# A second buffer for the turned block of an attention read, paid for with a buffer of the block it is made from

## The chip, the cores and the metric

The kernel runs on one core of one Trainium2 chip. The metric is the device time of one execution in microseconds (us). Before the change it is 499.29 us, the median of three runs (498.58 to 499.64). The engines are named as in the profile: PE is TensorE's matmul, PEld its weight load, DVE is VectorE, ACT is ScalarE, SP is SyncE, which here only issues transfers (SPq is its queue).

## What is computed

There are 8 batches with 8 heads, 512 tokens of 64 elements per head, and a state of 32 rows per head. Tokens read the state and the state reads the tokens, both by softmax attention; the 544 rows of each batch, with 512 columns, then go through a bilinear pair of weights and two more.

```python
scores = scale * np.matmul(x, state.transpose(0, 1, 3, 2))
a = np.exp(scores - scores.max(-1, keepdims=True)); a /= a.sum(-1, keepdims=True) + 1e-09
xread = np.matmul(a, state)
scores2 = scale * np.matmul(state, x.transpose(0, 1, 3, 2))
a2 = np.exp(scores2 - scores2.max(-1, keepdims=True)); a2 /= a2.sum(-1, keepdims=True) + 1e-09
sread = np.matmul(a2, x)
...
a = x @ w1
b = x @ w2
h = a * b @ w3
return (h @ w_out).astype(np.float32)
```

In the last four lines `x` is the concatenation of `xread` and `sread`, 8 x 544 rows of 512. Everything is float32.

## The kernel before

Each float32 operand of the large products is split in two parts that the matmul takes (`split`, lines 94 to 99: ACT writes the high part, DVE the low part), and a product is three matmuls, low by high, high by high, high by low.

**Prologue** (lines 510 to 617): the weights are loaded and converted, `w3` and `w_out` are multiplied into one matrix `wo`, and batch 0 is computed as the weights arrive. Batch 0's second stage runs at lines 622 to 630, with steps of batch 1's attention put between its pieces, among them the read of batch 0 (`reads[0]`). In the same stretch `combine_weights` (lines 362 to 373) is called four times, the last time at line 501 inside batch 1. It makes `t_hi` and `t_lo`, sums and differences of quarters of `wo`: two additions (L366), four subtractions (L372), then a split.

**Batches 1 to 7** (`quarter_batch`, lines 479 to 502): the first stage has eight groups, ft 0 to 7. Each is 12 matmuls of 128x512 (L311, in `stage1_sums`) into a pair of PSUM banks from the pool `ps_2`, which has three such pairs. ACT copies one half of the pair to SBUF (L487) and DVE multiplies the copy by the other half (L394). That multiplication is the last reader of the pair, so a later group can only start when it is done. Then the second stage (`stage2_quarters`, lines 427 to 477) makes seven products (L421) of the quarters, with the next batch's `sw` tiles (L147 and a split) between them.

**The attention of the next batch** runs inside a batch. After group ft = 1 (line 489) come, in this order: the read of the state for this batch (`read_state`, lines 234 to 257), the scores of the next batch (L147 into a `ps_2` pair that is held until its maximum, L190, its transposition, L187, and its exponentials, L197, are done), and the loads of the tokens of the next batch and of the x of the one after it (L159, L153, L155). The softmax's later steps are L204 to L228.

**The read of the state**, which the change touches: 64 small matmuls (L243) give a block of 128x128; DVE divides it by the softmax sum into the tile `scaled` (L248), transposes its 32x32 squares into the tile `turned` (L252), and 16 transfers of 4 KB on SP's queue (L171, `move_blocks`) carry `turned` into `sread`, 32 rows at a time. `sread` is used only at the end, in `state_rows`. The tiles come from the pool `att`, which has two buffers for each name unless `bufs=1` is given. So `scaled` had two buffers in turn and `turned` had one: a batch's transposition could write `turned` only after the 16 transfers of the batch before had read it.

**What sets the order.** PE's and SP's instructions run in the order in which they are written. From batch 0 on DVE and ACT are put in order when the kernel is built, by a scheduler that places instructions by its own estimate of when they can start. On the chip each engine's instructions start in the order that was built. On SP's queue the 16 transfers of batch 0's `turned` stand behind the 16 that move the softmax of batch 1 (`e<-work`, L171), although `turned` is written before; right behind them stand the 16 of batch 1's `turned`, and behind those the three loads.

Of the kernel before, what the change touches and what calls it, by code (L numbers as in the profile page):

```python
# [22 lines left out]
F32 = mybir.dt.float32  # L23
# [6 lines left out]
P = 128  # L30
# [9 lines left out]
def attn_bilinear_kernel(  # L40
# [11 lines left out]
    B, _, NT, H, D = x_s.shape  # L52
# [3 lines left out]
    KT = H * NS // P  # L56
# [10 lines left out]
    att = ctx.enter_context(tc.tile_pool(name="att", bufs=2))  # L67
# [20 lines left out]
    def bank():  # L88
        return ps_o.tile([P, NF], F32, name="ps_o")

    def two_banks():
        return ps_2.tile([P, 2, NF], F32, name="ps_2")

    def split(hi, lo, src):

        return (
            nc.scalar.copy(out=hi, in_=src),  # L97
            nc.vector.tensor_tensor(out=lo, in0=src, in1=hi.bitcast(F32), op=ALU.subtract),  # L98
        )
# [41 lines left out]
    def per_head(ps, b, moving):  # L141


        for j in range(NP):
            for q in range(KT):
                rows = slice(q * D, (q + 1) * D)
                nc.tensor.matmul(  # L147
                    ps[j * NS:(j + 1) * NS, q], sts[b][rows, j], moving(rows, j), start=True, stop=True
                )
# [14 lines left out]
    def work_tile():  # L164
        return att.tile([P, KT, S], F32, name="work")

    def move_blocks(dest, src):

        for j in range(NP):
            for c in range(P // NS):  # L170
                nc.sync.dma_start(  # L171
                    out=dest(slice(c * NS, (c + 1) * NS), j), in_=src(slice(j * NS, (j + 1) * NS), c)
                )

    def attention_steps(b):
        xd = x_tiles[b]
        a2 = {}

        def scores():

            ps = two_banks()
            per_head(ps, b, lambda rows, j: xd[rows, j])
            yield
            flat = lambda t: t.rearrange("p k s -> p (k s)")

            s1 = work_tile()
            nc.vector.transpose(out=flat(s1), in_=flat(ps))  # L187

            m2 = att.tile([P, KT], F32, name="m2")
            nc.vector.tensor_reduce(out=m2, in_=ps, axis=AX.X, op=ALU.max)  # L190
            nc.vector.tensor_scalar_mul(m2, m2, -SCALE)
            e2 = att.tile([P, KT, S], F32, name="e2", bufs=1)
            sum2 = att.tile([P, KT], F32, name="sum2")
            a2["e"], a2["sum"] = e2, sum2
            for kt in range(KT):
                one = slice(kt, kt + 1)
                nc.scalar.activation(  # L197
                    out=e2[:, kt], in_=ps[:, kt], func=AF.Exp, bias=m2[:, one], scale=SCALE, accum_out=sum2[:, one]
                )

            J = KT * S // NS
            s1v = flat(s1).rearrange("p (j n) -> p j n", n=NS)
            m1 = att.tile([P, J], F32, name="m1")
            nc.vector.tensor_reduce(out=m1, in_=s1v, axis=AX.X, op=ALU.max)  # L204
            nc.vector.tensor_tensor(
                out=s1v, in0=s1v, in1=m1.unsqueeze(2).broadcast_to([P, J, NS]), op=ALU.subtract
            )
            nc.scalar.activation(out=s1, in_=s1, func=AF.Exp, scale=SCALE)
            yield
            nc.vector.tensor_scalar_add(sum2, sum2, 1e-9)  # L210
            nc.vector.reciprocal(out=sum2, in_=sum2)
            sum1 = att.tile([P, J], F32, name="sum1")
            nc.vector.tensor_reduce(out=sum1, in_=s1v, axis=AX.X, op=ALU.add)
            nc.vector.tensor_scalar_add(sum1, sum1, 1e-9)
            nc.vector.reciprocal(out=sum1, in_=sum1)
            nc.vector.tensor_tensor(
                out=s1v, in0=s1v, in1=sum1.unsqueeze(2).broadcast_to([P, J, NS]), op=ALU.mult
            )
            yield
            at = work_tile()  # L220
            nc.vector.transpose(out=flat(at), in_=flat(s1))
            at_tiles[b] = [att.tile([P, KT, S], F32R, name=f"at_{part}", bufs=1) for part in ("hi", "lo")]
            last = split(*at_tiles[b], at)
            yield

            blocks = work_tile()
            with tc.issue_after(last[1].ins):
                nc.vector.transpose(out=flat(blocks), in_=flat(e2))  # L228
            a2["t"] = work_tile() if b < PLAIN else att.tile([P, KT, S], F32, name="e2", bufs=1)
            tiles = lambda t: t.rearrange("p k (t m) -> p (k t) m", m=P)  # L230
            move_blocks(lambda its, j: tiles(a2["t"])[its, :, j * NS:(j + 1) * NS],
                        lambda mine, c: tiles(blocks)[mine, :, c * NS:(c + 1) * NS])

        def read_state():

            xs = token_tiles[b]

            ps = (bank() if b else two_banks()[:, 0])[:, :KT * D].rearrange("p (k d) -> p k d", k=KT)
            for kt in range(KT):
                for t in range(NT):  # L240
                    for j in range(NP):
                        mine = slice(j * NS, (j + 1) * NS)
                        nc.tensor.matmul(  # L243
                            ps[mine, kt], a2["t"][:, kt, t * P + j * NS:t * P + (j + 1) * NS],
                            xs[:, t, 2 * j + kt], start=(t == 0), stop=(t == NT - 1),
                        )
            scaled = att.tile([P, KT, D], F32, name="scaled")
            a2["read"] = nc.vector.tensor_tensor(  # L248
                out=scaled, in0=ps, in1=a2["sum"].unsqueeze(2).broadcast_to([P, KT, D]), op=ALU.mult
            )  # L250
            turned = att.tile([P, KT, D], F32, name="turned", bufs=1)
            nc.vector.transpose(  # L252
                out=turned.rearrange("p k d -> p (k d)"), in_=scaled.rearrange("p k d -> p (k d)")
            )
            yield
            move_blocks(lambda its, j: sread[its, j, b * NS:(b + 1) * NS],
                        lambda mine, c: turned.rearrange("p k (c n) -> p (k c) n", n=NS)[mine, c])

        return scores, read_state, a2


# [446 lines left out]
```

## Time and profile before

| what | us |
|---|---|
| median of three runs (range) | 499.29 (498.58 to 499.64) |
| the profiled execution, its own time | 499.09 |
| its span in the trace | 497.3 |
| PE busy | 488.3 |
| DVE busy | 376.2 |
| ACT busy | 238.6 |

The span is the time from the first to the last instruction in the trace; 1.79 us of the profiled execution lie around it. All times within a trace count from the start of the span. A row of a timeline gives start, duration, engine, line, operation and tiles; a bracket at its end gives the idle time of the engine just before it and what ended that. In a row of waits stand who waited, for whom, the total, the number of times and the longest. Matmuls are pipelined: a 128x512 one is drawn 0.39 us long, and the next starts about 0.23 us after it.

### The profile page before, as it was taken

How to read it: one execution, taken by the hardware profiler on the slowest of the kernel's cores; microseconds unless marked ns; L12 is line 12 of the kernel's file. 1: busy time of each engine (PE TensorE's matmuls, PEld its weight loads, DVE VectorE, ACT ScalarE, POOL GpSimd, SP SyncE). 2: the span in 40 equal slices, each digit the busy share in tenths (PEclk: the TensorE clock that was granted, in tenths of full speed). 3: DMA queues.
4: the chain of work that ended last, by engine and by line, in shares of the span. 5: the costliest groups of instructions: out<-in, count | busy, mean ns of one | idle time of the engine just before them, and what ended most of it. 6: DMA issues, size and time to landing. Idle time of an engine off the chain costs nothing.

```text
span 497.3 us, 8933 instructions
## 1 busy us (share of the span) xinstructions
PE 488.3 (98%) x3558; PEld 379.4 (76%) x3558; DVE 376.2 (76%) x555; ACT 238.6 (48%) x364; POOL 0.2 (0%) x4
## 2 busy tenths in 40 slices
PE   8999999999989999999999999999999999999996
PEld 6444467777667978797879787978897789899885
DVE  5669896798689769956994799479938983577770
ACT  4777884454256225813570357045605550454650
POOL 0000000000000000000000000000000000000000
PEclk9999999999989999999999999999999999999999
DMA  8995971063013314140404041304130213001101
GB/s 341 366 415 198 368 267 30 13 217 73 21 48 133 81 51 144 44 99 25 176 12 119 5 178 33 97 4 176 44 86 5 88 44 84 6 3 47 39 2 42
DMA packets 56362, 52.50 MB, mean 106 GB/s; under 512 B 42752, under 2 KB 50944, under 8 KB 51712
## 3 DMA queue, kind: packets, MB, share of 16 engines
q1 hardware_dynamic: 47488, 43.27, 26.3%
q10 hardware_dynamic: 8832, 8.65, 5.1%
q8 instruction: 28, 0.46, 0.4%
q14 instruction: 14, 0.11, 0.1%
HBM read 38.27 MB, written 8.91 MB: 95 GB/s over the span
## 4 chain that ended last, share of the span: by engine, by line
PE 78%; DVE 10%; SPq 6%; ACT 3%; DMA 2%; issue 1%; DVEq 0%; ACTq 0%
PE ps L311 29%; PE ps_o L421 25%; SPq L171 6%; PE ps L147 6%; PE ps L421 4%; PE ps L647 3%; PE ps_o L528 3%; PE ps L528 3%; PE ps_o L325 3%; PE ps L648 2%; DVE w_sb L134 1%; PE ps_o L243 1%; DMA raw<-in_w_k_dram 1%; DVE sw_lo L98 1%; DVE w_sb L130 1%
## 5 line engine op out<-in xcount | busy, mean ns | idle before, releaser
L311 PE MATMUL ps<-at_lo,sw_hi 128*128 128x512 f32 x256 | 102.5, 401 | 3.4 <-DVE g_x L394 3.4
L311 PE MATMUL ps<-at_hi,sw_hi 128*128 128x512 f32 x256 | 100.4, 392 | 0.0
L311 PE MATMUL ps<-at_hi,sw_lo 128*128 128x512 f32 x256 | 100.3, 392 | 0.0
L487 ACT COPY tmp<-ps 128x512 f32<-128x512 f32 x56 | 32.8, 586 | 126.0 <-PE ps L311 71.8
L311 PEld LDWEIGHTS ps<-at_lo,sw_hi 128*128 128x128 f32 x256 | 48.4, 189 | 21.7 <-DVE g_x L394 11.0
L311 PEld LDWEIGHTS ps<-at_hi,sw_lo 128*128 128x128 f32 x256 | 48.4, 189 | 10.4
L311 PEld LDWEIGHTS ps<-at_hi,sw_hi 128*128 128x128 f32 x256 | 48.5, 190 | 9.7 <-issue 0.2
L394 DVE TENSOR_TENSOR g_x<-tmp,ps 128x512 f32<-128x512 f32 x28 | 19.1, 684 | 33.3 <-ACT tmp L487 32.8
L98 DVE TENSOR_TENSOR sw_lo<-ps,sw_hi 128x1024 fp32r<-128x1024 f32 (+1 forms) x34 | 38.0, 1151 | 0.2 <-ACT sw_hi L97 0.2
L97 ACT CAST g_hi<-g_x 128x512 fp32r<-128x512 f32 x42 | 26.0, 621 | 21.2 <-PE ps_o L421 13.1
L421 PE MATMUL ps_o<-t_lo,g_hi 128*128 128x256 f32 x168 | 34.5, 287 | 0.0
L421 PE MATMUL ps_o<-wo_lo,g_hi 128*128 128x256 f32 x168 | 34.4, 286 | 0.0
L421 PE MATMUL ps_o<-wo_hi,g_hi 128*128 128x256 f32 x168 | 33.8, 283 | 0.0
L421 PE MATMUL ps_o<-t_hi,g_hi 128*128 128x256 f32 x168 | 33.8, 283 | 0.0
L421 PE MATMUL ps_o<-wo_hi,g_lo 128*128 128x256 f32 x168 | 33.8, 283 | 0.0
L421 PE MATMUL ps_o<-t_hi,g_lo 128*128 128x256 f32 x168 | 33.8, 283 | 0.0
L97 ACT CAST g_hi<-raw 128x512 fp32r<-128x512 f32 x42 | 25.1, 619 | 16.8 <-DVE raw L394 7.7
L98 DVE TENSOR_TENSOR g_lo<-raw,g_hi 128x512 fp32r<-128x512 f32 x42 | 28.6, 687 | 5.1 <-ACT g_hi L97 4.8
L97 ACT CAST sw_hi<-ps 128x1024 fp32r<-128x1024 f32 (+1 forms) x34 | 31.1, 966 | 1.7 <-PE ps L147 1.6
L147 PE MATMUL ps<-w_sb,st 64*32 64x512 f32 (+1 forms) x544 | 31.4, 570 | 0.0
L421 PEld LDWEIGHTS ps_o<-wo_lo,g_hi 128*128 128x128 f32 x168 | 26.6, 191 | 5.6 <-ACT tmp L446 5.0
L421 PEld LDWEIGHTS ps_o<-t_lo,g_hi 128*128 128x128 f32 x168 | 26.1, 192 | 5.0 <-issue 5.0
(109 smaller groups left out, 895.3 us busy)
## 6 DMA issues: line engine op xcount, KB each, us to landing
raw<-in_w_k_dram SPq DMA_DIRECT2D x8, 1024.0 KB, 6.9
x_d<-in_x_d_dram SPq DMA_DIRECT2D x8, 1024.0 KB, 7.5
raw<-in_w_dram SPq DMA_DIRECT2D x8, 1024.0 KB, 6.3
x_s<-in_x_s_dram SPq DMA_DIRECT2D x8, 1024.0 KB, 5.1
out_dram<-tmp ACTq DMA_DIRECT2D x56, 128.0 KB, 1.8
raw<-in_w3t_dram SPq DMA_DIRECT2D x4, 1024.0 KB, 6.6
e<-work SPq DMA_DIRECT2D x112, 32.0 KB, 2.0
sread<-turned SPq DMA_DIRECT2D x128, 4.0 KB, 1.7
```

The costliest lines, as they stand in the source:

```text
L97: nc.scalar.copy(out=hi, in_=src),
L98: nc.vector.tensor_tensor(out=lo, in0=src, in1=hi.bitcast(F32), op=ALU.subtract),
L147: nc.tensor.matmul(ps[j * NS:(j + 1) * NS, q], sts[b][rows, j], moving(rows, j), start=True, stop=True)
L171: nc.sync.dma_start(out=dest(slice(c * NS, (c + 1) * NS), j), in_=src(slice(j * NS, (j + 1) * NS), c))
L311: nc.tensor.matmul(ps[:, i], w[:, kt, c:c + P], a[:, kt], start=(k == 0), stop=(k == 3 * KT - 1))
L325: nc.tensor.matmul(ps[:, :DO], g, wo[w][:, ft, :], start=(ft == 0 and k == 0), stop=(ft == FT - 1 and k == 2))
L394: nc.vector.tensor_tensor(out=whole, in0=a, in1=b, op=ALU.mult)
L421: nc.tensor.matmul(ps[:, tt * HO:(tt + 1) * HO], g[:, tt * P:(tt + 1) * P], w(part, k), start=(fresh and k == 0 and n == 0 and tt == 0), s ...
L487: nc.scalar.copy(out=a_sb, in_=ps[:, 0])
L528: nc.tensor.matmul(w34_ps[i][:, :DO], chunks[k][:, DO + i * P:DO + (i + 1) * P], w_out[k], start=(k == 0), stop=(k == FT - 1),)
L647: nc.tensor.matmul(ps[:, i], wh[:, ks], sr[:, kt], start=(kt == 0), stop=False)
L648: nc.tensor.matmul(ps[:, i, :n], wl[:, ks], sr[:, kt, 1], start=False, stop=(kt == NP - 1))
```

## The change

`scaled` gets one buffer instead of two and `turned` two instead of one. Both are blocks of 128x128 float32, so the pool takes as much room as before.

```diff
@@ read_state @@
-            scaled = att.tile([P, KT, D], F32, name="scaled")
+            scaled = att.tile([P, KT, D], F32, name="scaled", bufs=1)
             a2["read"] = nc.vector.tensor_tensor(
                 out=scaled, in0=ps, in1=a2["sum"].unsqueeze(2).broadcast_to([P, KT, D]), op=ALU.mult
             )
-            turned = att.tile([P, KT, D], F32, name="turned", bufs=1)
+            turned = att.tile([P, KT, D], F32, name="turned")
             nc.vector.transpose(
```

No instruction is added or taken away. On PE, ACT and SP the built order is the same as before, with the same waits. On DVE one instruction moves and the waits on transfers change.

The first place is on DVE in batch 1, from the last split before the read to the product of group ft = 3. `ps_1058` is the scores of batch 2, `ps_1084` and `ps_1114` are the banks of ft = 2 and ft = 3, and `[waits ...]` names the semaphores that an instruction waits for (DMAHW0 to DMAHW7 count transfers). Before:

```order
L98 TENSOR_TENSOR g_lo<-tmp,g_hi 128x512 [waits Activation_49]
L366 TENSOR_TENSOR tmp<-wo_hi,wo_lo 128x512 [waits DMAHW6_49]
L366 TENSOR_TENSOR tmp<-wo_hi,wo_lo 128x512 [waits DMAHW1_49]
L372 TENSOR_TENSOR raw<-tmp 128x256 [waits DVE_49] x2
L372 TENSOR_TENSOR raw<-tmp,raw 128x256 [waits DVE_49]
L187 STREAM_TRANSPOSE work<-ps_1058 128x1024 [waits PE_49]
L394 TENSOR_TENSOR g_x<-tmp,ps_1084 128x512 [waits Activation_49]
L252 STREAM_TRANSPOSE turned<-scaled 128x128 [waits DMAHW4_49,DMAHW5_49,DMAHW3_49,DMAHW6_49,DMAHW2_49,DMAHW7_49,DMAHW1_49,DMAHW0_49]
L372 TENSOR_TENSOR raw<-tmp,raw 128x256 [waits DVE_49]
L190 TENSOR_REDUCE m_1103<-ps_1058 128x2
L98 TENSOR_TENSOR t_lo<-raw,t_hi 128x4x256 [waits Activation_49]
L394 TENSOR_TENSOR g_x<-tmp,ps_1114 128x512 [waits Activation_49]
```

And after:

```order
L98 TENSOR_TENSOR g_lo<-tmp,g_hi 128x512 [waits Activation_49]
L252 STREAM_TRANSPOSE turned<-scaled 128x128 [waits DVE_49]
L366 TENSOR_TENSOR tmp<-wo_hi,wo_lo 128x512 [waits DMAHW6_49]
L366 TENSOR_TENSOR tmp<-wo_hi,wo_lo 128x512 [waits DMAHW1_49]
L372 TENSOR_TENSOR raw<-tmp 128x256 [waits DVE_49] x2
L372 TENSOR_TENSOR raw<-tmp,raw 128x256 [waits DVE_49]
L187 STREAM_TRANSPOSE work<-ps_1058 128x1024 [waits PE_49]
L394 TENSOR_TENSOR g_x<-tmp,ps_1084 128x512 [waits Activation_49]
L372 TENSOR_TENSOR raw<-tmp,raw 128x256 [waits DVE_49]
L190 TENSOR_REDUCE m_1103<-ps_1058 128x2
L98 TENSOR_TENSOR t_lo<-raw,t_hi 128x4x256 [waits Activation_49]
L394 TENSOR_TENSOR g_x<-tmp,ps_1114 128x512 [waits Activation_49]
```

The transposition L252 has moved seven instructions up, ahead of the last `combine_weights` and of the product of ft = 2, and waits for DVE's own `scaled` alone; the wait on all eight counts of transfers in front of L372 is gone.

The second place is on DVE later in batch 1, where the softmax of batch 2 is transposed back (L221). The piece of the difference:

```order
 L98 TENSOR_TENSOR g_lo_1307<-raw_1151,g_hi_1306 128x512
 L98 TENSOR_TENSOR sw_lo_1275<-ps_2_1265,sw_hi_1274 128x1024 [waits Activation_49]
-L221 STREAM_TRANSPOSE work_1338<-work_1101 128x1024
+L221 STREAM_TRANSPOSE work_1338<-work_1101 128x1024 [waits DMAHW4_49,DMAHW3_49,DMAHW5_49,DMAHW2_49,DMAHW7_49,DMAHW1_49,DMAHW0_49]
 L98 TENSOR_TENSOR g_lo_1391<-g_x_973,g_hi_1390 128x512 [waits PE_49,Activation_49]
 L98 TENSOR_TENSOR g_lo_1393<-g_x_1099,g_hi_1392 128x512 [waits PE_49,Activation_49]
```

Nothing moves here, but L221 now names seven counts of transfers itself, which the wait at L252 had covered for it before. In batches 2 to 7 L252 stands where it stood, without its waits on transfers.

## Prediction, on record before the run

> **What bounds the kernel now.** I read the page first, then the busy time by batch, then the waits, and last the timelines round the one wait that the change can touch.
>
> ```profile
> PE 488.3 (98%) x3558; PEld 379.4 (76%) x3558; DVE 376.2 (76%) x555; ACT 238.6 (48%) x364; POOL 0.2 (0%) x4
> ```
>
> PE is busy for 98% of the span, so time can be won only where PE idles or runs slowly. The busy time of each engine from one batch's read of the state (L243) to the next shows where that is; the columns after the stretch are its length, then busy us and instructions of PE, PEld, DVE, ACT and POOL, and PE's granted clock.
>
> ```profile
> 125.27:179.01 53.74, 50.39 (x413) 41.34 (x416) 41.46 (x62) 21.97 (x36) 0.00 (x0) 0.97 0.25 73
> 179.01:227.67 48.66, 48.66 (x413) 40.24 (x416) 38.01 (x55) 21.54 (x35) 0.00 (x0) 1.00 0.26 79
> 227.67:276.34 48.67, 48.67 (x412) 40.23 (x416) 37.92 (x55) 21.44 (x35) 0.00 (x0) 1.00 0.26 80
> ```
>
> Batch 1, the first row, issues the same matmuls as batch 2 and takes 53.74 us for 48.66, or 5.08 us more, with a clock below 1. That is a ceiling: nothing that mends batch 1 alone gains more. The list of waits says what ended its idle time.
>
> ```profile
> DVE turned L252 <- DMA sread<-turned: 2.8, 1, 2.8
> PE ps L311 <- DVE g_x L394: 3.4, 1, 3.4
> ```
>
> Only one of the eight transpositions into `turned` waited for the transfers of the batch before, for 2.8 us; and PE waited once for a product L394, for 3.4 us. The chain of waits joins the two.
>
> ```profile
> 133.75 1.72 DMA sread<-turned
> ...
> 135.59 0.31 DVE turned L252
> 135.90 0.31 DVE raw L372
> 136.21 1.14 DVE m L190
> 137.34 1.20 DVE t_lo L98
> 138.54 0.61 DVE g_x L394
> ...
> 139.20 10.06 PE ps L311 x36
> ```
>
> The last of batch 0's 16 small transfers lands, L252 runs, and four more DVE instructions stand between it and the product of group ft = 3 (L394), which frees the PSUM pair for group ft = 5. PE, at 139.20, starts that group.
>
> **The change part by part: the wait.** Here is DVE's timeline at that place.
>
> ```profile
> 132.11 0.65 DVE L394 TENSOR_TENSOR g_x<-tmp,ps 128x512 f32<-128x512 f32 x1
> 135.59 0.31 DVE L252 STREAM_TRANSPOSE turned<-scaled 128x128 f32<-128x128 f32 x1 [2.83 <-DMA sread<-turned]
> 135.82 0.38 DVE L372 TENSOR_TENSOR raw<-tmp,raw 128x256 f32<-128x256 f32 x1
> 138.46 0.68 DVE L394 TENSOR_TENSOR g_x<-tmp,ps 128x512 f32<-128x512 f32 x1
> 139.06 0.16 DVE L191 TENSOR_SCALAR m<-m 128x2 f32<-128x2 f32 x1
> ```
>
> A product L394 gives way to the next instruction after 0.60 us (138.46 to 139.06) and L252 after 0.23 (135.59 to 135.82). After the change L252 stands seven instructions higher. DVE has no idle time there (no bracket at 132.11), so its 0.23 us push the product of ft = 2 from 132.11 to 132.34. L372 follows it at 132.34 + 0.60 = 132.94 instead of 135.82: it comes **2.88 us** earlier. What hangs on L372 must come as much earlier, if ACT and PE let it:
>
> ```profile
> 136.24 1.04 ACT L97 CAST t_hi<-raw 128x1024 fp32r<-128x1024 f32 x1 [5.23 <-DVE raw L372]
> 137.19 0.58 ACT L487 COPY tmp<-ps 128x512 f32<-128x512 f32 x1
> ```
>
> ACT waited 5.23 us for L372 before the cast to `t_hi`, and behind that cast stands the copy of group ft = 3 (L487), at 137.19, then 134.31. PE's rows at the starts of groups ft = 2, 3, 5 and 6, and the last matmul of ft = 4, show whether that is too early:
>
> ```profile
> 127.32 0.50 PE L311 MATMUL ps<-at_lo,sw_hi 128*128 128x512 f32 x1
> 130.17 0.39 PE L311 MATMUL ps<-at_lo,sw_hi 128*128 128x512 f32 x1
> 135.46 0.39 PE L311 MATMUL ps<-at_hi,sw_lo 128*128 128x512 f32 x1
> 139.20 0.50 PE L311 MATMUL ps<-at_lo,sw_hi 128*128 128x512 f32 x1 [3.35 <-DVE g_x L394]
> 143.63 0.39 PE L311 MATMUL ps<-at_lo,sw_hi 128*128 128x512 f32 x1
> ```
>
> Group ft = 3 starts at 130.17 and 12 matmuls at about 0.23 us end it near 133, before 134.31. So the product of ft = 3 starts at 138.46 - 2.88 = 135.58 and PE may start ft = 5 at 139.20 - 2.88 = **136.32**. PE by itself would be ready at 135.46 + 0.23, and 0.23 later since ft = 4 waits for the pushed product of ft = 2: at 135.92. What is late next is thus the same product, by 0.40 us, still behind L372, L190 and the split of `t`; no new waiter takes its place.
>
> **The clock.** Of group ft = 5 the length is to be seen as well: 139.20 to 143.63 is 4.43 us, where ft = 2, which also starts after a wait, took 127.32 to 130.17, 2.85 us, for the same 12 matmuls. The stretches before, in and after it, with the granted clock third from the end:
>
> ```profile
> 135.80:139.20 3.40, 0.05 (x2) 0.00 (x1) 3.40 (x7) 1.55 (x3) 0.00 (x0) 1.00 0.05 7
> 139.20:143.40 4.20, 4.20 (x11) 3.30 (x12) 4.08 (x6) 2.42 (x6) 0.00 (x0) 0.59 0.05 6
> 143.40:149.10 5.70, 5.70 (x27) 4.69 (x25) 4.43 (x10) 3.16 (x5) 0.00 (x0) 1.00 0.32 93
> ```
>
> The clock granted was 0.59 after the 3.35 us of idle time and 1.00 again from 143.40. In the later batches the same place looks so:
>
> ```profile
> 229.65 0.19 PEld L311 LDWEIGHTS ps<-at_lo,sw_hi 128*128 128x128 f32 x1 [0.84 <-DVE g_x L394]
> 235.37 0.19 PEld L311 LDWEIGHTS ps<-at_lo,sw_hi 128*128 128x128 f32 x1 [0.41 <-DVE g_x L394]
> ```
>
> Waits of 0.84 and 0.41 us leave batch 3's clock at 1.00 (its row above). The 0.40 us that I leave to ft = 5 is of that size, so the clock stays up and the group takes 2.85 us: **1.58 us** more. [...]
>
> **The sum.** 2.88 + 1.58 = **4.46 us**, which leaves 0.62 of the ceiling of 5.08: the 0.40 and 0.2 that I do not place. It must then not be lost later. PE goes through ft = 5 to 7 by 4.46 us sooner, while DVE got only 2.88 from L372. DVE and ACT make it up because they wait for PE in that stage:
>
> ```profile
> 143.83 0.59 ACT L487 COPY tmp<-ps 128x512 f32<-128x512 f32 x1 [2.21 <-PE ps L311]
> 145.41 1.22 DVE L213 TENSOR_REDUCE sum<-work 128x32 f32<-128x1024 f32 x1 [0.19 <-ACT work L208]
> ```
>
> ACT waited 2.21 us for ft = 5 and DVE then for ACT, so from these on both follow PE. Between L372 and them ACT loses at most 4.46 - 2.88 = 1.58 of its 2.21 us of waiting. I see no loss to set against the sum: the order on PE, ACT and SP is unchanged, and the 0.23 us by which L252 pushes its successors is in it.
>
> **What costs nothing.** `scaled` with one buffer: L248 of a batch overwrites what L252 of the batch before has read, both on DVE, in order and some 50 us apart. L252 in batches 2 to 7 loses waits that took no time (the one wait in the row above is batch 1's). On SP's queue batch 1's 16 transfers no longer wait for L252 and follow batch 0's at SP's own pace, and the three loads behind them come with them:
>
> ```profile
> 135.93 0.51 SPq L171 DMA_DIRECT2D sread<-turned  x1
> 146.06 0.53 SPq L159 DMA_DIRECT2D x_s<-in_x_s_dram  x1
> 147.16 0.38 SPq L155 DMA_DIRECT2D x_d<-in_x_d_dram  x1
> x_d<-in_x_d_dram SPq DMA_DIRECT2D x8, 1024.0 KB, 7.5
> x_s<-in_x_s_dram SPq DMA_DIRECT2D x8, 1024.0 KB, 5.1
> ```
>
> SP issued batch 1's 16 from 135.93 to 146.06, 0.63 us each. Batch 0's last went out at 133.75, so batch 1's first can go at 134.38, 1.55 us before 135.93. The loads move as much, to 144.5 and 145.6, and land about 149.6 and 153.1. That is 2.9 us less than PE gains, but the tokens are wanted only at the read of batch 2 (179.01 before, 174.55 after): 25 us of cover.
>
> The sum against the profiled execution is 499.09 - 4.46 = 494.63. The median of the runs is 0.20 above that execution, which would make 494.83. I say **494.7**.
>
> **The rivals.**
>
> *The clock's part is lost again.* DVE had 41.46 us of work in batch 1 against 38.01 in batch 2, and if ACT or DVE is later than I work out, PE waits in ft = 6, ft = 7 or the first products for what it gained at full clock. Then only the first term stays: 499.09 - 2.88 = 496.2. For it: DVE is nearly full between 135.59 and 149. Against it: the waits for PE just quoted. 8%.
>
> *The clock falls in the profiled execution but not in all.* The idle time of 3.35 us may be just at the limit, so that the runs without a profile were at full clock already and owe their time to something else; the gain is then 2.88 against the median, 499.29 - 2.88 = 496.4. For it: only one fall of the clock is in the trace, so its limit is not known. [...] Against: the three runs lie within 1.06 us, less than 1.58, on both sides of the profiled one. 6%.
>
> *Nothing comes of it.* If PE's wait were due to something that L252's wait only hid, such as the split of `t` held by another transfer, the time stays at 499.1 to 499.3. Against: every link from L252 to PE is in the chain above without idle time. That the change doesn't do what it says I rule out: the built order shows the wait gone. 3%.
>
> *Slower: L221 inherits a wait that lasts.* It now names seven counts of transfers itself, and behind it on DVE stands the split that a later product needs:
>
> ```profile
> 158.23 1.23 DVE L221 STREAM_TRANSPOSE work<-work 128x1024 f32<-128x1024 f32 x1
> 159.39 1.25 DVE L98 TENSOR_TENSOR g_lo<-g_x,g_hi 128x512 fp32r<-128x512 f32 x2
> 165.22 0.40 PE L421 MATMUL ps<-t_hi,g_lo 128*128 128x256 f32 x2
> ```
>
> L221 would be due at 158.23 - 4.46 = 153.77. The first of the two splits ends at about 160.1 and PE takes it at 165.22, so 5.1 us of delay are covered. If the counts included the load of `x_d`, which lands at 153.1 by the median, it would just pass. At 20 us instead of 7.5 to landing it would hold L221 to 165.6, 11.8 us; PE would idle 6.7 and lose another 1.58 to the clock: 494.63 + 8.3 = 502.9. It decides from a hold of 9 us, about where the idle time with the clock's fall (3.9 + 1.58) eats the gain and 1 us more. Against: what L221 must wait for is the 16 transfers that read the tile it overwrites, issued ahead of the ones whose last landed at 135.47 (133.75 + 1.72, in the chain). 2%.
>
> **How the numbers follow.** The forecast has the 81% that are left. Its own range is 494.0 (the ceiling of 5.08) to 495.2 (0.5 us of waits that I place wrongly). The runs before lie from 0.51 below the profiled time to 0.55 above, which makes 493.5 at the bottom. At the top the first two rivals are taken in, to 496.5. The chances go by 0.2%, 1.0 us, about what a measurement of this kernel can tell from no change: the forecast and the first two rivals are faster (0.81 + 0.08 + 0.06 = 0.95), the third is the same (0.03), the last slower (0.02).
>
> **What would show it.** Right: no wait of L252 for transfers; L252 near 128.7; PE idle about 0.4 us ahead of ft = 5, near 136.3; a clock of 1.00 through that group; batch 1 from L243 to L243 about 49.3 us; `x_s` issued near 144.5. Wrong: a wait of over 1 us for L394 or a clock below 1 in batch 1, or a wait of L221 for a transfer. A batch 1 of about 50.9 us would be the first rival; one of 49.3 with a time of 496.4 the second.

## The result, and the profile after

The changed kernel takes 494.83 us (median of five runs, 494.38 to 494.94), the kernel before 499.29 us (498.58 to 499.78 in five). The ratio is 0.991 with a 95% interval of 0.9895 to 0.9924, so 4.46 us or 0.9% faster. The profiled execution took 494.89 us, its span is 493.1 us. In the experiments one execution of the kernel before took 688.31 us, at a mean granted clock of 0.656; it is left out of every number below.

Batch 1 and batch 2 of the changed kernel, in the busy time by stretch (length, then busy us and instructions of PE, PEld, DVE, ACT and POOL, PE's granted clock, DMA share, GB/s):

```profile
125.66:174.87 49.21, 48.95 (x413) 40.22 (x416) 41.17 (x62) 21.96 (x36) 0.00 (x0) 1.00 0.27 80
174.87:223.51 48.64, 48.64 (x412) 40.22 (x416) 38.01 (x55) 21.54 (x35) 0.00 (x0) 1.00 0.26 79
136.66:139.51 2.85, 2.85 (x12) 2.36 (x13) 2.85 (x5) 2.42 (x6) 0.00 (x0) 1.00 0.04 6
```

Batch 1 went from 53.74 to 49.21 us and stands 0.57 above batch 2; the last row is its group ft = 5, 2.85 us at full clock. DVE's timeline at the place of the wait (the second row begins the product of ft = 2, the last one that of ft = 3):

```profile
129.11 0.31 DVE L252 STREAM_TRANSPOSE turned<-scaled 128x128 f32<-128x128 f32 x1
...
132.68 0.65 DVE L394 TENSOR_TENSOR g_x<-tmp,ps 128x512 f32<-128x512 f32 x1
133.25 0.41 DVE L372 TENSOR_TENSOR raw<-tmp,raw 128x256 f32<-128x256 f32 x1
...
135.92 0.68 DVE L394 TENSOR_TENSOR g_x<-tmp,ps 128x512 f32<-128x512 f32 x1
```

None of these rows has a bracket: L252 ran with no wait, and L372 follows the product of ft = 2 at once. PE's and its weight load's idle time ahead of groups ft = 4 and ft = 5:

```profile
133.39 0.19 PEld L311 LDWEIGHTS ps<-at_lo,sw_hi 128*128 128x128 f32 x1 [0.37 <-DVE g_x L394]
136.66 0.19 PEld L311 LDWEIGHTS ps<-at_lo,sw_hi 128*128 128x128 f32 x1 [0.68 <-DVE g_x L394]
136.66 0.50 PE L311 MATMUL ps<-at_lo,sw_hi 128*128 128x512 f32 x1 [0.26 <-DVE g_x L394]
```

The 3.35 us of PE's idle time ahead of ft = 5 have become 0.26; the first two rows are the weight load's, which waits longer than PE. Later in the batch L221, which took over the named waits, starts without one:

```profile
154.07 1.25 DVE L221 STREAM_TRANSPOSE work<-work 128x1024 f32<-128x1024 f32 x1
```

SP's first load behind batch 1's transfers of `turned`, at 146.06 before:

```profile
144.81 0.53 SPq L159 DMA_DIRECT2D x_s<-in_x_s_dram  x1
```

The span fell by 4.2 us, a little less than batch 1 did (4.53), because in this execution the read of batch 1 began 0.39 us later (125.66 for 125.27). In the other profiles below that read begins between 124.8 and 126.0, in no order that goes with the edits. That the loads of the prologue make the difference is a guess; no run shows it.

### The profile page after: what moved, and what is told of

The parts are those of the page before. It is cut to its first block, busy times and chain, and to the rows that moved or that the text cites. A ratio compares the mean times of both kernels' runs of the same rounds, so it can differ in the third digit from the quotient of the medians.

```text
span 493.1 us, 8917 instructions
## 1 busy us (share of the span) xinstructions
PE 486.8 (99%) x3558; PEld 378.4 (77%) x3558; DVE 375.9 (76%) x555; ACT 238.8 (48%) x364; POOL 0.2 (0%) x4
## 4 chain that ended last, share of the span: by engine, by line
PE 77%; DMA 7%; DVE 7%; ACT 5%; SPq 2%; issue 1%; DVEq 0%; ACTq 0%
PE ps L311 30%; PE ps_o L421 25%; PE ps L147 6%; PE ps_o L325 5%; PE ps L421 4%; DMA raw<-in_w_k_dram 3%; PE ps L647 3%; ACT ulps L126 2%; SPq L171 2%; DMA raw<-in_w_dram 2%; PE ps L648 2%; DMA raw<-in_w3t_dram 2%; PE ps_o L243 1%; ACT w_sb L118 1%; DVE work L187 1%
## 5 line engine op out<-in xcount | busy, mean ns | idle before, releaser
L311 PE MATMUL ps<-at_lo,sw_hi 128*128 128x512 f32 x256 | 101.9, 398 | 0.3 <-DVE g_x L394 0.3
L311 PE MATMUL ps<-at_hi,sw_hi 128*128 128x512 f32 x256 | 99.8, 390 | 0.0
L311 PE MATMUL ps<-at_hi,sw_lo 128*128 128x512 f32 x256 | 99.7, 389 | 0.0
L311 PEld LDWEIGHTS ps<-at_lo,sw_hi 128*128 128x128 f32 x256 | 48.1, 188 | 18.7 <-DVE g_x L394 8.1
L311 PEld LDWEIGHTS ps<-at_hi,sw_lo 128*128 128x128 f32 x256 | 48.1, 188 | 10.2
L311 PEld LDWEIGHTS ps<-at_hi,sw_hi 128*128 128x128 f32 x256 | 48.1, 188 | 9.5 <-issue 0.2
L394 DVE TENSOR_TENSOR g_x<-tmp,ps 128x512 f32<-128x512 f32 x28 | 19.1, 683 | 33.3 <-ACT tmp L487 32.8
```

What stands on the lines that cost most here:

```text
L311: nc.tensor.matmul(ps[:, i], w[:, kt, c:c + P], a[:, kt], start=(k == 0), stop=(k == 3 * KT - 1))
L394: nc.vector.tensor_tensor(out=whole, in0=a, in1=b, op=ALU.mult)
```

## The experiments

The theory: the second buffer of `turned` removes the wait at L252; that is worth the 2.9 us by which PE starts ft = 5 sooner, and 1.6 us more because PE's clock then does not fall. The rivals: `scaled` or the place of L252 has a part; the slow matmuls come from something other than the idle time; the clock falls in some executions only. All medians, with the kernel before on the same chip; "low clock" counts the executions with a mean granted clock of 0.997 or less. That mean takes in the last microseconds too, in which PE has nothing left to do. In the profile of the changed kernel, with a mean of 0.998, the clock is below 1.00 only there (0.81 from 489.20 us to the end), so 0.998 is no sign of slow matmuls. In that of the kernel before, with 0.997, it fell in batch 1 alone (0.66 from 139.00 to 144.00); in that of e1_both_one, with 0.995, it fell in batch 1 too (0.63 from 138.75 to 143.40).

| kernel | us | low clock | before, us | ratio (95%) |
|---|---|---|---|---|
| e1_both_one | 498.96 | 11 of 12 | 498.90 | 1.0012 (0.9994 to 1.0030) |
| e2_fill_12 | 499.19 | 0 of 12 | 498.90 | 1.0011 (0.9994 to 1.0029) |
| e3_fill_5 | 496.80 | 1 of 9 | 498.48 | 0.9974 (0.9960 to 0.9989) |
| e4_fill_2 | 497.85 | 5 of 10 | 498.48 | 0.9987 (0.9972 to 1.0002) |
| e5_read_first | 501.86 | 6 of 6 | 498.90 | 1.0069 (1.0042 to 1.0096) |
| e6_place | 494.38 | 0 of 6 | 498.90 | 0.9922 (0.9898 to 0.9947) |
| e7_after_again | 494.77 | 0 of 6 | 498.62 | 0.9925 (0.9903 to 0.9948) |
| e8_combine_ft2 | 494.96 | 0 of 6 | 498.62 | 0.9932 (0.9911 to 0.9952) |
| e9_combine_early | 495.24 | 0 of 6 | 498.62 | 0.9936 (0.9916 to 0.9956) |

**e1_both_one: the change's other half alone.**

```diff
-            scaled = att.tile([P, KT, D], F32, name="scaled")
+            scaled = att.tile([P, KT, D], F32, name="scaled", bufs=1)
...
             turned = att.tile([P, KT, D], F32, name="turned", bufs=1)
```

> One buffer for both tiles. My theory (the second buffer of `turned` takes away the wait at L252; `scaled` never needed its second): as the kernel before, L252 again behind the product of ft = 2 with a wait of about 2.8 us, PE idle 3.35 us ahead of group ft = 5, that group about 4.4 us long, 499.3 us in all (498.6 to 499.9). Rival, that the single buffer of `scaled` or the shifted tile addresses had a part in the gain or cost something: a time away from 499.3 by more than 0.6 us.

It ran as the kernel before, 498.96 us to 498.90. Its list of waits and its timeline on PE, from ft = 5 on:

```profile
DVE turned L252 <- DMA sread<-turned: 2.4, 1, 2.4
```

```profile
138.75 0.50 PE L311 MATMUL ps<-at_lo,sw_hi 128*128 128x512 f32 x1 [2.98 <-DVE g_x L394]
...
140.01 0.63 PE L311 MATMUL ps<-at_hi,sw_lo 128*128 128x512 f32 x1
140.43 0.63 PE L311 MATMUL ps<-at_lo,sw_hi 128*128 128x512 f32 x1
...
143.42 0.40 PE L311 MATMUL ps<-at_hi,sw_hi 128*128 128x512 f32 x1
143.66 0.40 PE L311 MATMUL ps<-at_hi,sw_lo 128*128 128x512 f32 x1
```

The wait is back, and so is the fall of the clock: start to start of matmuls goes from 0.23 to 0.43 us. It begins at about 140.0, 1.2 us after the idle time was over, and lasts to 143.4. So the single buffer of `scaled` costs nothing that the runs can tell, and the second of `turned` does it all. A kernel with two buffers of each was not run.

**e2_fill_12, e3_fill_5, e4_fill_2: the clock without the wait's removal.** In the kernel before:

```diff
+            if b == PLAIN and ft == 5:
+                spare = bank()
+                for n in range(12):
+                    nc.tensor.matmul(spare, wo["hi"][:, 0, :P], at_tiles[b][0][:, 0], start=True, stop=True)
             ps = stage1_sums(b, ft)
```

(5 and 2 in place of 12 in the other two.)

> The kernel before, with 12 matmuls of 128x512 whose result is never read put on PE between groups ft = 4 and ft = 5 of batch 1, so that PE works through most of its 3.35 us of waiting. The wait at L252 stays. My theory (2.9 us of the gain are the wait, 1.6 us are PE's clock, which falls after the idle time): PE idle about 0.6 us there, group ft = 5 2.85 us long at a clock of 1.00, and 499.3 - 1.6 = 497.7 us in all, if the new order that the scheduler gives DVE behind this place costs nothing (497.2 to 498.6). Rival, that the whole gain is the wait and the slow matmuls come from something else in the stage (the load of DVE and ACT at that time): group ft = 5 still about 4.4 us and 499.3 us in all.

> The kernel before with 5 instead of 12 matmuls put into PE's wait ahead of group ft = 5 of batch 1; their result is never read. PE then idles 3.35 - 5 x 0.23, about 2.2 us, in one piece. If the clock falls only after an idle time near 3.4 us: group ft = 5 2.85 us at a clock of 1.00, 497.7 us. If it falls sooner: group ft = 5 above 3.5 us and 498.7 us or more.

> The kernel before with 2 matmuls put into PE's wait ahead of group ft = 5 of batch 1; their result is never read. PE idles about 2.9 us in one piece. [...]

The stretch of group ft = 5 in the three, with the granted clock third from the end: first e2_fill_12, then e3_fill_5, then e4_fill_2.

```profile
138.56:141.40 2.84, 2.84 (x12) 2.36 (x13) 2.84 (x5) 2.42 (x6) 0.00 (x0) 1.00 0.05 6
```

```profile
139.36:142.20 2.84, 2.84 (x12) 2.36 (x13) 2.84 (x5) 2.43 (x6) 0.00 (x0) 1.00 0.04 6
```

```profile
138.75:143.60 4.85, 4.85 (x14) 3.87 (x15) 4.82 (x9) 3.99 (x9) 0.00 (x0) 0.65 0.05 6
```

And the start of ft = 5 in e3_fill_5 and in e4_fill_2, with PE's idle time in the bracket:

```profile
139.36 0.50 PE L311 MATMUL ps<-at_lo,sw_hi 128*128 128x512 f32 x1 [1.70 <-DVE g_x L394]
```

```profile
138.75 0.50 PE L311 MATMUL ps<-at_lo,sw_hi 128*128 128x512 f32 x1 [2.50 <-DVE g_x L394]
...
140.29 0.63 PE L311 MATMUL ps<-at_lo,sw_hi 128*128 128x512 f32 x1
```

The wait at L252 is still there, 2.3 us in the first two and 2.4 in the third; its row in e3_fill_5:

```profile
DVE turned L252 <- DMA sread<-turned: 2.3, 1, 2.3
```

With it there, work put into PE's idle time keeps the clock at 1.00 in the profiles of e2_fill_12 and e3_fill_5 and makes 12 matmuls take 2.84 us instead of 4.43: the slow matmuls come from the idle time, and the rival that blamed the stage falls. In whole times only e3_fill_5 shows it: its median is 1.7 us below the one before, where I had 1.6, and by the interval of the ratio the gain is between 0.5 and 2.0 us. PE idled 1.70 us there where I had 2.2, since L252 waited less than in the profile I had reckoned from. e2_fill_12 gave it back, which I had not foreseen: with 12 matmuls more in PE's row the scheduler puts DVE's later work in another order, and one wait of PE in the second stage is new:

```profile
157.45 1.09 PE L147 MATMUL ps<-w_sb,st 64*32 64x512 f32 x16 [1.58 <-DVE sw_lo L98]
```

So 1.6 us went from one wait to another and the whole stayed. In e4_fill_2 I had held it likelier, 65 to 35, that the clock stays up. It fell in the profile, after 2.50 us idle, and in 5 of 10 executions; those five have a median of 498.81 us, the others 496.94.

**e5_read_first: the wait removed without a second buffer.** In the kernel before:

```diff
         def rest():
-            with tc.issue_after(stored[0].ins):
-                yield from softmax
             yield from read
+            with tc.issue_after(stored[0].ins):
+                yield from softmax
```

> The kernel before (one buffer for `turned`), with batch 0's 16 transfers of `turned` issued on SP ahead of the 16 that move batch 1's softmax instead of behind them. My theory: the wait at L252 goes without a second buffer, since those transfers land near 117, but the softmax's are issued until about 126 and land near 128, so that PE waits for them at the read of the state (L243) for about 3.1 us, on the edge of what made the clock fall; 494.8 + 3.1 = 497.9 us, or 499.4 if the clock falls as well. Rival, that a wait of L252 would stay whatever the order on SP: L252 waits over 1 us for transfers again.

The order on SP does take the wait away, but the whole is 501.86 us, 3.0 slower than before and 2.5 above the worse of my two figures. SP's timeline, then DVE's at L252 and PE's at the read of the state:

```profile
104.20 13.98 SPq L171 DMA_DIRECT2D sread<-turned  x16
118.30 10.46 SPq L171 DMA_DIRECT2D e<-work  x16
```

```profile
132.65 0.30 DVE L252 STREAM_TRANSPOSE turned<-scaled 128x128 f32<-128x128 f32 x1
```

```profile
125.69 0.27 PE L243 MATMUL ps_o<-x_s,e 128*32 128x64 f32 x2 [0.56 <-DMA e<-work]
127.75 0.39 PE L243 MATMUL ps_o<-x_s,e 128*32 128x64 f32 x2 [1.79 <-DMA e<-work]
130.19 1.89 PE L243 MATMUL ps_o<-x_s,e 128*32 128x64 f32 x58 [2.04 <-DMA e<-work]
```

And two stretches, one before the last of these waits is over and one behind it, with PE's busy time behind the length and the clock third from the end:

```profile
127.60:130.10 2.50, 0.39 (x2) 0.18 (x2) 1.78 (x3) 0.02 (x1) 0.00 (x0) 0.50 0.28 45
130.19:136.00 5.81, 5.81 (x82) 3.66 (x83) 3.76 (x8) 1.05 (x1) 0.00 (x0) 0.64 0.03 6
```

L252 has no wait, as I expected. My size for the other side was wrong: SP needed 0.87 us for each of the 16 (13.98 us) where I had 0.63, so the softmax's transfers ended at 128.8 instead of 126. PE waited 0.56 + 1.79 + 2.04 = 4.39 us where I had 3.1, and all six executions have a low clock. In the profile it was at 0.50 from 127.6, towards the end of the second wait, until 134.4, and 0.64 is its mean over the 5.8 us behind the waits. Of the two orders on SP's queue, the one that takes L252's wait away costs more at the read of the state than it saves; that is what makes the second buffer worth having. An order that mixes the two sets of transfers, or a second queue for one of them, was not tried.

**e6_place: the wait or the place.** In the changed kernel, for batch 1 alone:

```diff
             a2["read"] = nc.vector.tensor_tensor(
...
+            if b == PLAIN:
+                yield
             turned = att.tile([P, KT, D], F32, name="turned")
```

with the rest of the read, and the loads behind it, run at ft = 2 instead of ft = 1.

> The changed kernel (two buffers for `turned`), with L252 of batch 1 written behind the product of ft = 2; the scheduler then puts L252 and the last L372 ahead of L187 and that product, four instructions later than in the changed kernel. The order on PE, ACT and SP is that of the changed kernel. My theory (the wait is what counts, the place is worth tenths): no wait at L252, the product of ft = 2 some 0.3 us later, PE idle 0.3 to 1 us ahead of ft = 4 and ft = 5, clock 1.00, 495.1 us (494.6 to 495.8). Rival, that it is L252's place ahead of `combine_weights` that gains: above 497 us.

494.38 us, a little under the range I had, and no wait at L252. PE's weight load, ahead of ft = 4 and ft = 5 (two lines of code more: L313 is L311 of the changed kernel, L396 its L394):

```profile
133.87 0.19 PEld L313 LDWEIGHTS ps<-at_lo,sw_hi 128*128 128x128 f32 x1 [0.70 <-DVE g_x L396]
136.74 0.19 PEld L313 LDWEIGHTS ps<-at_lo,sw_hi 128*128 128x128 f32 x1 [0.25 <-DVE g_x L396]
```

The two idle times of the weight load have changed places (0.37 and 0.68 in the changed kernel) and their sum is nearly the same, 0.95 us for 1.05. So L252's place does not matter; the wait does. The 0.4 us between this median and those of the changed kernel are within the spread of either, on different chips: I make nothing of them.

**e7_after_again, e8_combine_ft2, e9_combine_early: what is left.** The first is the changed kernel as it is. The other two move the last `combine_weights`:

```diff
-            if b == PLAIN and ft == 1:
+            if b == PLAIN and ft == 2:
                 combine_weights(QF - 1)
```

```diff
-            if b == PLAIN and ft == 1:
+            if b == PLAIN and ft == FT:
                 combine_weights(QF - 1)
...
-        if tt + 1 < QF:
+        if tt < QF:
             combine_weights(tt)
```

> The changed kernel once more, for its clock in many executions and for comparison on one chip with the next two. In the kernel before the clock has fallen in about five of six executions and not in the others, 1.6 to 2.2 us apart. My theory (the changed kernel's longest wait of PE in batch 1 is too short for the clock to fall): the mean clock is 0.998 or more in every execution, the times lie within about 1 us of each other, 494.2 to 495.2. Rival, that the clock's fall depends on the moment and hits the changed kernel too: some executions at 0.997 or less and 1.6 us longer.

> The changed kernel with the last `combine_weights` written behind group ft = 2 of batch 1 instead of ft = 1, to see whether the 0.5 us that batch 1 still takes above batch 2 can be had. In the built order its two L366 and two of its L372 stand between L205 and the product of ft = 3. From the steady batches that product would then start about 1.7 us later than there and PE would wait about 1 us ahead of ft = 5, at full clock: 495.1 us (494.5 to 495.7), no gain. Rival, that its place was what cost the 0.5 us: 494.3 us.

> The changed kernel with the last `combine_weights` called behind batch 0's last stored piece, not in batch 1. The product of ft = 0 of batch 1 then stands behind two L366 and two L372, and that of ft = 1 behind the last L372 and the split of `t` that waits for ACT. I expect the product of ft = 1 about 3 us later than now (129 for 126.4), PE idle about 2 us ahead of ft = 2, the clock falling in some executions only, as with 1.7 to 2.5 us of idle time so far, and batch 1 otherwise like batch 2: 496.3 us without the fall and 497.9 with it. Rival, that DVE has room there and the 0.5 us are won: 494.3 us.

The changed kernel kept its clock at 0.999 or more in all six executions, 494.38 to 495.09 us. Neither move is faster on the same chip. The wait only goes elsewhere; e8_combine_ft2, then e9_combine_early:

```profile
142.13 0.47 PE L311 MATMUL ps<-at_lo,sw_hi 128*128 128x512 f32 x1 [0.94 <-DVE raw L394]
```

```profile
134.74 0.50 PE L311 MATMUL ps<-at_lo,sw_hi 128*128 128x512 f32 x1 [1.49 <-DVE g_x L394]
```

In the first I had a wait of about 1 us ahead of ft = 5; PE waits 0.94 us, but two groups later, ahead of ft = 7. In the second I had 2 us ahead of ft = 2 and 496.3 us. The product of ft = 1 comes at 128.94, as I had it, but ft = 2 had started at 127.51 and did not need it; the wait is 1.49 us ahead of ft = 4 and costs less (495.24 us). It never brought the clock down in six executions. No version tried beats the changed kernel by more than the runs can tell.

## Why the prediction was right

**The wait, 2.88 us.** From the read of batch 1 to the start of ft = 5 it was 139.20 - 125.27 = 13.93 us and is 136.66 - 125.66 = 11.00: 2.93. The steps in between hold one by one: L252 pushes the product of ft = 2, the weight load waits 0.37 us ahead of ft = 4, PE waits a little ahead of ft = 5, still for the product of ft = 3, and nothing new comes late. One reading was wrong and changes nothing in the sum: three DVE instructions, not four, stand between L252 and the product of ft = 3.

The size, though, is that of one execution. The wait at L252 was 2.83 us in the profile I worked from and 2.3 to 2.4 in those of e1_both_one and the three filled kernels, and PE idled 2.98 us in e1_both_one for 3.35. My sum with an idle time shorter by that 0.37 us is 4.09. Between the rows of L243 in PE's timelines batch 1 took 53.67 us before (125.27 to 178.94), 53.32 in e1_both_one (125.21 to 178.53) and 49.14 in the changed kernel (125.66 to 174.80), so the gain against e1_both_one is 4.18 us and not 4.53.

**The clock, 1.58 us.** Group ft = 5 took 4.43 us and takes 2.85: 1.58. The runs with filled idle time show that this is the idle time's doing and apart from the wait itself. To show that the clock stays at 1.00 I had compared PE's 0.40 us with waits of 0.84 and 0.41 us that had left it there. Those are rows of the weight load, which waits longer than PE (3.77 us before ft = 5 where PE idled 3.35). Like set beside like, the weight load waits 0.68 us there in the changed kernel, still under 0.84, so the step held.

**The two together.** Batch 1 is 4.53 us shorter where I had 4.46, takes 49.21 us where I had 49.3, and nothing of it is lost later. SP issues the load of `x_s` 1.25 us earlier in the span, 1.64 if the later start is taken off, where I had 1.55, and PE notices nothing of that.

**The rivals.** That DVE and ACT lag behind did not come: ft = 6 and 7 show no wait of PE. L221 has no wait. The rival on the clock I had dealt with too lightly. I argued from three runs that the fall is in every execution; it is not. Over the 50 executions of the kernel before that stand beside the experiments, on two chips, 39 have a mean clock of 0.997 or less, 497.88 to 500.23 us with a median of 498.86; the other 11 have 1.00, 496.62 to 498.38 with a median of 497.01. The changed kernel has none below 0.998 in 11. So my forecast for the changed kernel was right because the changed kernel's clock is steady, and its distance from the median before was right because most executions before have the fall. Against the ones without it the change is worth about 2.2 us (497.01 to 494.77), against the ones with it about 4.1 (498.86 to 494.77), close to the 4.09 of the shorter idle time. Whether the executions without a fall had a shorter wait still is not shown, since none of them has a profile.

That the median came out 4.46 us lower, to the last digit what I had, is luck. The five executions of the kernel before beside this result have a median of 499.29 us, the 50 later ones 498.71, and the changed kernel, measured again, was 3.85 us faster than the kernel before on the same chip (498.62 to 494.77). The two terms and their causes stand; about 3.9 us is the better figure for the gain.

That the clock falls only after an idle time near 3.4 us, the first case in the expectation of e3_fill_5, the runs do not bear out: 2.50 us were enough in e4_fill_2, and in e5_read_first the clock fell when no idle time had been longer than 1.79 us. In the three profiles with a fall behind one idle time in batch 1 (before, e1_both_one, e4_fill_2) it begins 0.7, 1.2 and 1.4 us after the idle time is over, at a different matmul in each, and lasts 3.4 us (140.0 to 143.4 in e1_both_one); in e5_read_first it lasts twice that (127.6 to 134.4). The same idle time also need not end alike, as the last section shows.

## What to carry to other kernels

A tile with one buffer that is emptied by transfers can make its next writer wait for those transfers and for all that stand in front of them on the queue, here 32 small ones together. It did so in one of eight batches, for 2.83 us in the profile before. Look at which work stands behind that writer on its engine, since it was not the transposition that cost time but the product four instructions later. And count an idle time of PE of 2.5 us or more at more than its own length: the fall of the clock that may follow cost 1.6 us more here, in half of the executions at 2.5 us and in four of five near 3.

## What the runs showed of the hardware

Where PE's idle time was in one piece, the clock fell the more often the longer it was. With the idle time of PE from one profile of each kernel:

| PE idle in the profile, us | executions with a low clock |
|---|---|
| 2.98 to 3.35 (before, e1_both_one) | 50 of 62 |
| 2.50 (e4_fill_2) | 5 of 10 |
| 1.70 (e3_fill_5) | 1 of 9 |
| 1.49 (e9_combine_early) | 0 of 6 |
| 0.26 (changed kernel, with e7_after_again) | 0 of 11 |

The profile gives the idle time of one execution; the same wait gave 3.35 us in the kernel before and 2.98 in e1_both_one, so the steps of the table are not sharp. The length in one piece is not all that counts. In the profile of e5_read_first PE had idled 0.56 us and then, behind two small matmuls, 1.6 us of a wait of 1.79 when the clock fell at 127.6; all six executions of that kernel have a low clock.

Nor does the same idle time always end alike. Behind the last matmuls of the changed kernel, which start at 488.56 us in its own profile and have ended by 489.20, the stretches to the end of the span are these, first in the changed kernel's own profile (two rows), then in e7_after_again (one):

```profile
489.20:491.50 2.30, 0.00 (x0) 0.00 (x0) 0.00 (x0) 0.59 (x1) 0.00 (x0) 1.00 0.34 94
491.70:493.00 1.30, 0.00 (x0) 0.00 (x0) 0.00 (x0) 0.00 (x0) 0.00 (x0) 0.50 0.02 5
489.20:493.00 3.80, 0.00 (x0) 0.00 (x0) 0.00 (x0) 0.58 (x1) 0.00 (x0) 1.00 0.26 69
```

In the first the clock went to 0.50 at 491.60, about 2.4 us behind the last matmul; in the second it was at 1.00 through all 3.80 us.

A kernel whose times fall into two groups on one core, as the kernel before does with medians 1.85 us apart (497.01 and 498.86), may have an idle time behind which the clock falls in some executions and not in others, here in 39 of 50; the mean granted clock of each execution helps to tell the groups apart (0.997 or less and 1.00 here).

SP's pace for the same 4 KB transfers was 0.63 us each in the kernel before (16 from 135.93 to 146.06) and 0.87 us in e5_read_first, where they follow the three loads of the next batch at once. Whether the loads slow the issue was not tried.
